# Stores of the gated results: issued by ScalarE with the next gate instead of by GpSimd

## The chip, the cores and the metric

One Trainium2 chip, one of its cores. The metric is the device time of one execution in microseconds (us); the median of three runs stands for a kernel. Engines are named as the profile names them: PE is TensorE (PEld its weight loads), DVE is VectorE, ACT is ScalarE, POOL is GpSimd, SP is SyncE. A "q" behind a name (SPq, ACTq, POOLq) is the engine's sequencer, which issues DMAs.

## The reference, cut to what matters

Linear attention with a decaying state over 4 x 768 tokens and 8 heads of 64, then two feed-forward stages on the 3072 x 512 result. All data are float32 or wider.

```python
state = gamma * state + k[t] v[t]^T ;  y[t] = scale * q[t] @ state     # attention
a = x @ w1 ; b = x @ w2                                                 # 512 -> 1024
h = a * b @ w3 ; x = h @ w_out                                          # 1024 -> 1024 -> 512
h = x @ w_in ; g = h * sigmoid(1.702 * h) ; out = g @ w_out2            # 512 -> 2048 -> 512
```

The change lies around the gate `a * b`, while its results are written to DRAM for the product with `w3 @ w_out`, which the kernel has multiplied into one matrix.

## The kernel before

**Tiling.** Every float32 operand is split into a high and a low float32r part, and each product is three matmuls (`mm3`, lines 245 to 248). The 3072 tokens are six blocks of 512; the gate is computed block by block in the order 0, 2, 4, 1, 3, 5 (`ORDER`). A block has eight gates `t` = 0 to 7, one per 128 rows of the 1024. A gate (`gate_mm`) is 24 matmuls of 128x512 into two PSUM tiles `ab` (`a` and `b`), taken from a pool of six (`mm`, `bufs=6`), so three gates fit in PSUM.

**What happens to a gate.** `gate_out` (lines 283 to 285) copies `ab[0]` to SBUF on ACT and multiplies by `ab[1]` on DVE. The product that follows is a seven-product block scheme (Strassen's kind), which needs sums and differences of blocks. Blocks 0, 2, 4 only store their gates (`gate_first`). Blocks 1, 3, 5 form differences with the stored ones (`gate_second`, lines 1011 to 1025). The eight gates of such a block make four pairs. The even gate of a pair gives `b12` (ACT copy, DVE product) and one difference `g[:, 1]` (DVE, line 1018). The odd gate gives `g[:, 0]`, then `g[:, 3]` on DVE (line 1021), `g[:, 2]` and `g[:, 4]` on POOL (lines 1022, 1023), and the DMA of the whole tile `g` (5 x 512 floats in each of 128 partitions, 1280 KB) to `hd` in DRAM, issued by POOL (line 1024). There are 3 x 4 = 12 pairs; here they are called p1 to p12, p1 to p4 of block 1, p5 to p8 of block 3, p9 to p12 of block 5. The tile `g` has two buffers: p3 can be written only when the store of p1 has landed.

**What runs beside it.** The order of every engine is the order in which the program calls it. Between the matmuls of a gate and `gate_second`, `work(n)` puts in `n` steps that convert the weights of the last stage: ACT takes the magnitude (line 128), DVE does eight operations on two tiles (lines 183 to 205), and then `seven` gives POOL four sums and differences (`four`, line 159) and three stores (line 148). ACT also casts the high part of the next block's `x` (`split`, line 261) and DVE its low part (line 162). SP issues the loads: `h` of the next pair (line 1008, into one of two buffers that POOL's line 1023 reads last), raw weights (line 118), `x` (line 266). At the end of block 5, `opening` and `blend` load the stored blocks again (`l`, `h` from `hd`, line 796) and the product with the mixed matrix begins (PSUM tiles `m`).

In the program each DMA that SP or ACT issues takes one of eight semaphores in turn, and so does each DMA of POOL, from another eight; a DMA waits until the earlier one on its semaphore has landed.

Of the kernel before, what the change touches and what calls it, by code (L numbers as in the profile page):

```python
# [24 lines left out]
KD, KF, KG = DM // P, DF // P, DG // P  # L25
# [18 lines left out]
def tile_kernel(  # L44
# [14 lines left out]
    nc = tc.nc  # L59
# [15 lines left out]
    def spool(name, n, *shape):  # L75
        return [dram.tile(shape, F32, name=f"{name}{i}", tag=f"{name}{i}") for i in range(n)]

    xd = spool("xd", NB, CPB, P, KD, P)
    hd = spool("hd", NB // 2, P, NM, 7, TB)
# [86 lines left out]
    def seven(i, a1, a2):  # L166
        st = (
            st_ready.pop()
            if st_ready
            else homes["st"].tile([P, 1024], F32, tag="st", bufs=2, name="st")  # L170
        )
        four(st, a1, a2)
        store_parts(i, a1, a2, st)
# [66 lines left out]
    def weight(i):  # L240
        while complete <= i:
            work(1)
        return parts[i]

    def mm3(ps, wh, wl, xh, xl, start, stop):
        nc.tensor.matmul(ps, wh, xh, start=start, stop=False, skip_group_check=True)  # L246
        nc.tensor.matmul(ps, wh, xl, start=False, stop=False, skip_group_check=True)  # L247
        nc.tensor.matmul(ps, wl, xh, start=False, stop=stop, skip_group_check=True)  # L248
# [15 lines left out]
    def reload(key, d):  # L264
        lo = x_tiles(key)[1][:, d].bitcast(F32)
        nc.sync.dma_start(
            lo.rearrange("p (c t) -> p c t", c=CPB), xd[key][:, :, d].rearrange("c p t -> p c t")
        )

    def split_x(key, d):  # L270
        hi, lo = (t[:, d] for t in xhl[key])
        split(hi, lo, lo.bitcast(F32))

    def gate_mm(t, key, tile):
        w = [x.rearrange("p (m k f) -> p m k f", m=2, k=KD) for x in weight(t)]
        xh, xl = xhl[key]
        ab = [tile() for _ in range(2)]
        for m, ps in enumerate(ab):
            for d in range(KD):
                mm3(ps, w[0][:, m, d], w[1][:, m, d], xh[:, d], xl[:, d], d == 0, d == KD - 1)  # L280
        return ab

    def gate_out(out, ab):
        nc.scalar.copy(out, ab[0])
        nc.vector.tensor_tensor(out, out, ab[1], ALU.mult)

    def h_tile():
        return xs.tile([P, 2, TB], F32, tag="h", bufs=2, name="h")
# [525 lines left out]
    def opening(t):  # L814
        if t:
            name = blends[t - 1][1]
            wm[name] = wtile("wg")
            nc.sync.dma_start(
                wm[name][1].bitcast(F32), sm[PART[name]].rearrange("p k c -> p (k c)")
            )  # L820
        if t == 1:
            x = spare.tile([P, 7, TB], F32R, tag="ope", name="h0")
            hi2[0] = x[:, NM:]
            load_h(0, 0, NM, x[:, :NM])
        if t == KF - 2:
            for k in (0, 2):
                load_h(1, k, k + 2, prep.tile([P, 2, TB], F32R, tag="r", bufs=R_BUFS, name="h1"))
        if t in (3, 4, 5):
            split_h(0, t - 3, t - 2, hi2[0][:, t - 3 : t - 2])
        if t == 6:  # L830
            hi2["k3"] = prep.tile([P, TB], F32R, tag="x", bufs=6, name="h3")
            split_h(0, 3, 4, hi2["k3"].rearrange("p (a t) -> p a t", a=1))
        if t in (4, 6):
            split_wm(t // 2 - 2)
# [77 lines left out]
    with tc.manual_schedule():  # L912
# [54 lines left out]
        with (  # L967
            tc.tile_pool(name="ps1", bufs=1, space=PSUM, reuse_waits="tile") as psb,
            ExitStack() as stage,
        ):  # L970
            pb = stage.enter_context(tc.tile_pool(name="b1", bufs=1, reuse_waits="tile"))
            homes.update(dict.fromkeys(("wa", "wc", "st"), pb))
            limit = ALL

            def mixed_bank():
                return psb.tile([P, DM], F32, tag="w", bufs=2, name="psw")

            psw = mixed_bank()
            rows = 0
            pair = None  # L980

            def mix_mm(f):
                h3, l3 = (x.rearrange("p (k f) -> p k f", k=KF) for x in weight(W3 + f))
                ps = psw if f == 0 else mixed_bank()
                for k in range(KF):
                    ho, lo = (
                        x.rearrange("p (k f) -> p k f", k=2)[:, k % 2]
                        for x in weight(WO + k // 2)
                    )
                    mm3(ps, h3[:, k], l3[:, k], ho, lo, k == 0, k == KF - 1)  # L990
                return ps

            def mix_out(f, ps):
                nonlocal pair
                if f % 2 == 0:
                    pair = pb.tile([P, 2, 2, 256], F32, tag="xp", bufs=2, name="xp")
                nc.scalar.copy(pair[:, :, f % 2], ps.rearrange("p (m f) -> p m f", m=2))
                if f % 2:
                    seven(f // 2, *(pair[:, m].rearrange("p a f -> p (a f)") for m in range(2)))

            def gate_tile():
                return psb.tile([P, TB], F32, tag="mm", bufs=6, name="psm")

            hb = []

            def load_b(i, k):
                t = h_tile()
                nc.sync.dma_start(t, hd[i // 2][:, k, :2])
                hb.append(t)

            def gate_second(t, i, ab):
                nonlocal b12, g
                b = hb[0]
                if t % 2 == 0:
                    b12 = first_b.pop() if first_b else b12_tile()
                    g = pb.tile([P, 5, TB], F32, tag="g", bufs=2, name="g")
                    gate_out(b12, ab)
                    nc.vector.tensor_tensor(g[:, 1], b12, b[:, 0], ALU.subtract)
                    return
                gate_out(g[:, 0], ab)  # L1020
                nc.vector.tensor_tensor(g[:, 3], g[:, 0], b12, ALU.subtract)
                nc.gpsimd.tensor_tensor(g[:, 2], g[:, 0], g[:, 1], ALU.subtract)
                nc.gpsimd.tensor_tensor(g[:, 4], b[:, 1], g[:, 2], ALU.subtract)
                nc.gpsimd.dma_start(hd[i // 2][:, t // 2, 2:], g)
                hb.pop(0)

            def b12_tile():
                return pb.tile([P, TB], F32, tag="b", bufs=2, name="b12")

            b12 = g = None  # L1030
            for n, i in list(enumerate(ORDER))[1:]:
                nxt = ORDER[n + 1] if n + 1 < NB else None
                for t in range(KF):
                    if nxt is None:
                        opening(t)
                    elif t < 2:
                        for d in range(2):
                            reload(nxt, 2 * t + d)
                    if n > 2 and t % 2 == 0 and t + 2 < KF:
                        load_b(i, t // 2 + 1)  # L1040
                    if n >= 2 and nxt is not None and t == KF - 2:
                        load_b(nxt, 0)
                    ab = gate_mm(t, i, gate_tile)
                    if nxt is not None and t in range(KD - 1, KF - 1):
                        split_x(nxt, t - KD + 1)
                    work(((8, 6, 3, 3)[n - 1] + (n < 4) * (t % 2)) if n < 5 else (t < 4) + (t < 5))
                    (gate_second if n > 2 else gate_first)(t, i, ab)
                    while rows < KF and (complete > W3 + rows or (n, t) == (2, KF - 1)):
                        ps = mix_mm(rows)
                        work(7)  # L1050
                        mix_out(rows, ps)
                        rows += 1
                        if rows == KF:
                            stage.close()
                            pb = homes["st"] = stage.enter_context(
                                tc.tile_pool(name="b2", bufs=1, reuse_waits="tile")
                            )
                            st_ready = [pb.tile([P, 1024], F32, tag="st", bufs=2, name="st")]
                            first_b = [b12_tile()]
                            pb.tile([P, 1024], F32, name="gap")  # L1060
        inner.close()
        homes["st"] = second.enter_context(
            tc.tile_pool(name="wa", bufs=1, side="right", reuse_waits="tile")
# [135 lines left out]
```

## Time and profile before

| | us |
|---|---|
| median of 3 runs | 980.32 |
| lowest and highest | 978.99, 987.53 |
| the profiled execution | 985.11 |
| its span, first to last instruction | 983.3 |
| PE busy in the span | 965.2 |
| DVE, ACT, POOL busy | 714.1, 444.0, 205.6 |

The profile is one execution. Its own time is 985.11 us, of which 983.3 us are the span that all views show; 1.81 us lie around it. Times in the rows are microseconds from the span's start. The stage of the change, from the first `g` to the last store, runs from about 275 to 404 us.

### The profile page before, as it was taken

Reading aid. Unit: us, or ns where it says so; the run is one execution under the profiler, and the core shown is the slowest. Engines: PE = TensorE matmul, PEld = TensorE weight load, DVE = VectorE, ACT = ScalarE, POOL = GpSimd, SP = SyncE. Lnnn points to the kernel's source line nnn. Section 1 sums busy time; section 2 is a strip of 40 time slices with the busy share of each in tenths; the row PEclk is TensorE's granted clock in tenths of the full one; section 3 lists DMA queues with packets and bytes.
Section 4 is the critical chain, followed back from the end, with each engine's and each line's share of the span. In section 5 each row is a group of like instructions: output and inputs, shape, how many; then the busy total and the mean of one; then the engine's idle time right before and its main releaser. Section 6 shows DMA issues by size and latency. Waiting matters only on the chain.

```text
span 983.3 us, 14857 instructions
## 1 busy us (share of the span) xinstructions
PE 965.2 (98%) x5608; PEld 836.4 (85%) x5608; DVE 714.1 (73%) x965; ACT 444.0 (45%) x787; POOL 205.6 (21%) x248
## 2 busy tenths in 40 slices
PE   6999999999999999999999999999999999999998
PEld 5788878888888888778889999999999888888886
DVE  4878878888898896675786895867777475567662
ACT  5666644443322222455446744545545544354430
POOL 5010000278785875240110000000000000000000
PEclk9999999999999999999999999999999999999999
DMA  9889955669898989978767647465596968767871
GB/s 360 336 330 352 356 207 197 216 232 339 315 324 326 347 311 367 404 269 295 271 238 288 250 169 278 180 227 230 197 363 251 331 227 286 243 195 247 287 236 54
DMA packets 115288, 268.73 MB, mean 273 GB/s; under 512 B 8000, under 2 KB 69440, under 8 KB 106128
## 3 DMA queue, kind: packets, MB, share of 16 engines
q1 hardware_dynamic: 100688, 193.98, 56.3%
q0 software_dynamic: 14384, 73.61, 19.3%
q8 instruction: 44, 0.72, 0.3%
q14 instruction: 28, 0.23, 0.1%
q10 hardware_dynamic: 144, 0.20, 0.1%
HBM read 165.52 MB, written 102.24 MB: 272 GB/s over the span
## 4 chain that ended last, share of the span: by engine, by line
PE 89%; DVE 5%; DMA 2%; ACT 1%; issue 1%; POOL 0%; DVEq 0%; ACTq 0%; POOLq 0%
PE m L247 11%; PE m L248 11%; PE m L246 11%; PE psm L246 7%; PE psm L248 7%; PE psm L247 7%; PE a L247 4%; PE a L246 4%; PE a L248 4%; PE y L404 2%; PE s L354 2%; PE e L246 2%; PE e L248 2%; PE e L247 2%; PE psg L246 2%; DMA l<-hd 2%
## 5 line engine op out<-in xcount | busy, mean ns | idle before, releaser
L246 PE MATMUL psm<-xh,wh 128*128 128x512 f32 x320 | 124.6, 389 | 0.0
L248 PE MATMUL psm<-xh,wl 128*128 128x512 f32 x320 | 124.5, 389 | 0.0
L247 PE MATMUL psm<-xl,wh 128*128 128x512 f32 x320 | 124.5, 389 | 0.0
L246 PE MATMUL m<-h,op 128*128 128x512 f32 x320 | 124.5, 389 | 0.0
L248 PE MATMUL m<-h,op 128*128 128x512 f32 x320 | 124.5, 389 | 0.0
L247 PE MATMUL m<-l,op 128*128 128x512 f32 x304 | 118.3, 389 | 0.0
L685 ACT CAST h<-l 128x2048 fp32r<-128x2048 f32 x38 | 72.3, 1914 | 82.8 <-PE m L248 57.4
L686 DVE TENSOR_TENSOR l<-l,h 128x2048 fp32r<-128x2048 f32 x38 | 85.6, 2286 | 20.8 <-ACT h L685 20.8
L247 PE MATMUL a<-yl,op 128*128 128x384 f32 x256 | 85.6, 335 | 0.1
L246 PE MATMUL a<-yh,op 128*128 128x384 f32 x256 | 85.6, 334 | 0.0
L248 PE MATMUL a<-yh,op 128*128 128x384 f32 x256 | 85.5, 334 | 0.0
L691 POOL DMA_DIRECT2D op<-sw x6 | 3.2, 532 | 393.1 <-PE a L248 212.8
L128 ACT ACTIVATE x<-raw 128x512 f32<-128x512 f32 x72 | 46.4, 671 | 75.3 <-DMA raw<-in_wo_dram 43.9
L246 PEld LDWEIGHTS m<-h,op 128*128 128x128 f32 x320 | 60.1, 188 | 12.6
L248 PEld LDWEIGHTS psm<-xh,wl 128*128 128x128 f32 x320 | 60.1, 188 | 12.6
L247 PEld LDWEIGHTS psm<-xl,wh 128*128 128x128 f32 x320 | 60.1, 188 | 12.5
L248 PEld LDWEIGHTS m<-h,op 128*128 128x128 f32 x320 | 60.1, 188 | 12.4
L246 PEld LDWEIGHTS psm<-xh,wh 128*128 128x128 f32 x320 | 60.1, 188 | 12.4 <-issue 0.2
L247 PEld LDWEIGHTS m<-l,op 128*128 128x128 f32 x304 | 57.1, 188 | 11.7
L246 PE MATMUL m<-h,wh 128*128 128x512 f32 x168 | 66.0, 393 | 0.2 <-ACT h L261 0.2
L162 DVE TENSOR_TENSOR l<-l,h 128x2048 fp32r<-128x2048 f32 x19 | 43.6, 2292 | 30.9 <-ACT h L261 30.1
L248 PE MATMUL m<-h,wl 128*128 128x512 f32 x168 | 65.9, 392 | 0.0
(165 smaller groups left out, 2209.5 us busy)
## 6 DMA issues: line engine op xcount, KB each, us to landing
gd<-g SPq DMA_DIRECT2D x32, 1344.0 KB, 4.7
qkv<-in_qkv_dram POOLq DMA_DIRECT2D x20, 1024.0 KB, 8.8
l<-gd SPq DMA_DIRECT2D x26, 768.0 KB, 6.8
l<-hd SPq DMA_DIRECT2D x19, 1024.0 KB, 6.5
raw<-in_w_dram SPq DMA_DIRECT2D x30, 512.0 KB, 5.0
hd<-g POOLq DMA_DIRECT2D x12, 1280.0 KB, 9.1
raw<-in_wo_dram SPq DMA_DIRECT2D x24, 512.0 KB, 7.0
l<-gd SPq DMA_DIRECT2D x24, 512.0 KB, 5.3
```

What stands on the lines that cost most here:

```text
L128: nc.scalar.activation(x, high, AF.Abs, scale=2.0**16)
L162: nc.vector.tensor_tensor(lo, x, hi.bitcast(F32), ALU.subtract)
L246: nc.tensor.matmul(ps, wh, xh, start=start, stop=False, skip_group_check=True)
L247: nc.tensor.matmul(ps, wh, xl, start=False, stop=False, skip_group_check=True)
L248: nc.tensor.matmul(ps, wl, xh, start=False, stop=stop, skip_group_check=True)
L354: nc.tensor.matmul(sc[c][j][:, p, :], qkt[c][r, 1, p, :], qkt[c][r, 0, p, :], start=True, stop=True,)
L404: nc.tensor.matmul(out_y, vs[c][:, 2 * p + j, :], pt[c][:, j, p, :], start=(p < 2), stop=first, skip_group_check=True,)
L685: nc.scalar.copy(hi, x.bitcast(F32))
L686: nc.vector.tensor_tensor(x, x.bitcast(F32), hi.bitcast(F32), ALU.subtract)
L691: queue.dma_start(t.bitcast(F32), sw[PART[name]])
```

## The change

The DMA of `g` is no longer issued in `gate_second` by POOL. It is put in a list, `unstored`, and issued by ACT in the next pair's even gate, right behind ACT's copy of `b12` and DVE's product. The last pair of all (`nxt is None and t == KF - 1`) keeps POOL, and is issued at once behind the loop over blocks.

```diff
-            hb = []
+            hb, unstored = [], []
+
+            def store_g():
+                while unstored:
+                    queue, to, x = unstored.pop()
+                    queue.dma_start(to, x)
...
                     gate_out(b12, ab)
+                    store_g()
                     nc.vector.tensor_tensor(g[:, 1], b12, b[:, 0], ALU.subtract)
                     return
...
                 nc.gpsimd.tensor_tensor(g[:, 4], b[:, 1], g[:, 2], ALU.subtract)
-                nc.gpsimd.dma_start(hd[i // 2][:, t // 2, 2:], g)
+                unstored.append((nc.gpsimd if nxt is None and t == KF - 1 else nc.scalar, hd[i // 2][:, t // 2, 2:], g))
                 hb.pop(0)
...
+            store_g()
         inner.close()
```

Lines behind the change have other numbers in the changed kernel: 1008 becomes 1013, 1018 becomes 1024, 1021 to 1023 become 1027 to 1029, and the store, 1024, becomes 1009.

ACT's order in pairs p4 to p6 before (`b_` is an even gate's copy, `g` an odd gate's, `x` a weight's magnitude, `xh` the cast of the next block):

```order
L284 COPY b_3289<-psm 128x512
L128 ACTIVATE x<-raw 128x512 x2
L284 COPY g<-psm 128x512
L284 COPY b_3381<-psm 128x512
L128 ACTIVATE x<-raw 128x512 x2
L284 COPY g<-psm 128x512
L284 COPY b_3470<-psm 128x512
L261 CAST xh<-xl 128x512
```

ACT's order in the same place after:

```order
L284 COPY b_3288<-psm 128x512
L1009 DMA hd_77<-g 128x2560
L128 ACTIVATE x<-raw 128x512 x2
L284 COPY g<-psm 128x512
L284 COPY b_3380<-psm 128x512
L1009 DMA hd_77<-g 128x2560
L128 ACTIVATE x<-raw 128x512 x2
L284 COPY g<-psm 128x512
L284 COPY b_3469<-psm 128x512
L1009 DMA hd_78<-g 128x2560
L261 CAST xh<-xl 128x512
```

The three DMAs are the stores of p3, p4 and p5; each stands between the even copy of the pair after it and two magnitudes or a cast.

POOL's order from the end of p3 to the start of p4 before (`st` and `sw` are the weight work of `seven`):

```order
L1023 TENSOR_TENSOR g<-h,g 128x512
L1024 DMA hd_77<-g 128x2560
L159 TENSOR_TENSOR st<-x 128x256
L159 TENSOR_TENSOR st<-st,x 128x256
L159 TENSOR_TENSOR st<-x 128x256
L159 TENSOR_TENSOR st<-x,st 128x256
L148 DMA sw_98<-x 128x2x256
L148 DMA sw_98<-x 128x256
L148 DMA sw_98<-st 128x4x256
L1022 TENSOR_TENSOR g<-g 128x512
```

POOL's order in the same place after:

```order
L1029 TENSOR_TENSOR g<-h,g 128x512
L159 TENSOR_TENSOR st<-x 128x256
L159 TENSOR_TENSOR st<-st,x 128x256
L159 TENSOR_TENSOR st<-x 128x256
L159 TENSOR_TENSOR st<-x,st 128x256
L148 DMA sw_98<-x 128x2x256
L148 DMA sw_98<-x 128x256
L148 DMA sw_98<-st 128x4x256
L1028 TENSOR_TENSOR g<-g 128x512
```

Only the DMA of `g` is gone; everything else stands as it stood. SP's and DVE's instructions and their order are the same in both kernels, and PE's too.

## Rows read from the trace of the kernel before

**Rows 1.** The page, busy time, share of the span, instructions of each engine.

```profile
PE 965.2 (98%) x5608; PEld 836.4 (85%) x5608; DVE 714.1 (73%) x965; ACT 444.0 (45%) x787; POOL 205.6 (21%) x248
```

**Rows 2.** Busy time by stretch; at the end granted clock, DMA share, GB/s.

```profile
core 0: us, PE busy (x) PEld busy (x) DVE busy (x) ACT busy (x) POOL busy (x), PEclk, DMA share, GB/s
270.00:300.00 30.00, 30.00 (x134) 24.86 (x133) 26.72 (x34) 6.20 (x12) 23.77 (x27) 1.00 0.96 342
300.00:320.00 20.00, 20.00 (x90) 16.57 (x89) 18.80 (x24) 6.04 (x11) 12.76 (x16) 1.00 0.81 305
320.00:340.00 20.00, 20.00 (x89) 16.54 (x89) 17.87 (x21) 5.60 (x10) 16.29 (x18) 1.00 1.00 356
...
410.00:415.00 5.00, 3.60 (x9) 2.88 (x10) 3.68 (x4) 0.93 (x2) 0.00 (x0) 0.66 1.01 403
```

**Rows 3.** Waits of PE, 265 to 425 us: total, times, longest.

```profile
PE m L247 <- DVE l L162: 2.5, 2, 1.8
```

**Rows 4.** The store's line 1024: its wait, who waited for it, its landing.

```profile
L1024 POOL DMA_DIRECT2D hd<-g x12: 555/564/712, 285.7 to 403.2; - x12
...
  POOL g L1023: 3.6, 12
...
  ACT g L284: 19.6, 3
  DVE g L1018: 7.4, 4
...
DMA to landing us min/median/max: 7.5/9.1/10.9
```

**Rows 5.** DMA issues of the whole run: size, median us from issue to landing.

```profile
gd<-g SPq DMA_DIRECT2D x32, 1344.0 KB, 4.7
```

**Rows 6.** The one DMA that ACT issues: duration of the issue, ns.

```profile
L744 ACTq DMA_DIRECT2D out_dram<-c x1: 370/370/370, 980.4 to 980.4; - x1
```

**Rows 7.** Timeline of POOL, pairs p3 to p5: start, us, and idle before.

```profile
310.50 1.35 POOL L1023 TENSOR_TENSOR g<-h,g 128x512 f32<-128x512 f32 x1
312.14 0.56 POOL L1024 DMA_DIRECT2D hd<-g  x1 [0.30 <-POOL g L1023]
315.66 0.85 POOL L159 TENSOR_TENSOR st<-x 128x256 f32<-128x256 f32 x1 [2.96 <-DVE x L205]
...
322.71 1.63 POOL L1023 TENSOR_TENSOR g<-h,g 128x512 f32<-128x512 f32 x1
...
333.21 1.62 POOL L1023 TENSOR_TENSOR g<-h,g 128x512 f32<-128x512 f32 x1
```

**Rows 8.** Timeline of ACT, pairs p2 to p6.

```profile
286.44 0.66 ACT L128 ACTIVATE x<-raw 128x512 f32<-128x512 f32 x1 [9.68 <-DMA raw<-in_wo_dram]
...
302.80 0.59 ACT L284 COPY b<-psm 128x512 f32<-128x512 f32 x1 [0.36 <-PE psm L248]
...
308.29 0.59 ACT L284 COPY g<-psm 128x512 f32<-128x512 f32 x1 [1.04 <-PE psm L248]
...
321.94 0.57 ACT L284 COPY g<-psm 128x512 f32<-128x512 f32 x1
324.56 0.59 ACT L284 COPY b<-psm 128x512 f32<-128x512 f32 x1 [2.06 <-PE psm L248]
325.05 0.62 ACT L261 CAST xh<-xl 128x512 fp32r<-128x512 f32 x1
332.57 0.59 ACT L284 COPY g<-psm 128x512 f32<-128x512 f32 x1 [6.90 <-DMA hd<-g]
...
363.17 1.23 ACT L128 ACTIVATE x<-raw 128x512 f32<-128x512 f32 x2
```

**Rows 9.** Timeline of PE: two matmuls that stand 24 apart.

```profile
269.96 0.39 PE L246 MATMUL psm<-xh,wh 128*128 128x512 f32 x1
...
275.40 0.39 PE L246 MATMUL psm<-xh,wh 128*128 128x512 f32 x1
```

**Rows 10.** The chain that ended last: the end of the gates.

```profile
397.74 0.24 PE psm L248
```

## The prediction

> **What bounds the kernel now.** I read the page's busy times first. TensorE (PE) is busy for 965.2 of 983.3 us [rows 1], so a change gains only what PE waits, and loses only what PE is made to wait. Next come the stretches of the stage: from 270 to 340 us PE is busy all the time at full granted clock, while ScalarE (ACT) is busy 6.20 of 30 us, 6.04 of 20 and 5.60 of 20, and VectorE (DVE) 26.72 of 30, 18.80 of 20 and 17.87 of 20 [rows 2]. PE's own waits between 265 and 425 us are 2.5 us in two places [rows 3], and both are after the gates, at the first products with reloaded blocks. Around them the granted clock from 410 to 415 us is 0.66 [rows 2]: 5 x 0.34 = 1.7 us are lost to the lower of the two levels. So the stage has 4.2 us to give at most, and only if the loads at its end come sooner.
>
> **PE's timetable.** All else is measured against it. Two matmuls that stand 24 apart start 5.44 us apart [rows 9]: one gate. The last of the 24 gates of p1 to p12 ends at 397.74 + 0.24 = 397.98 [rows 10]; without idle time, gate n ends at 397.98 - (24 - n) x 5.44. With six PSUM tiles, two a gate, gate n + 3 begins 10.88 us after gate n ends, and by then ACT must have copied gate n; DVE's product has 2.72 us more, 13.60. That cover is real: ACT sat idle for 9.68 us before 286.44 [rows 8], and PE stayed busy for all 30 us around it [rows 2].
>
> **What the change removes.** Eleven issues on GpSimd (POOL) go, each 564 ns behind a gap of 3.6 / 12 = 0.30 us [rows 4]: 11 x 0.86 = 9.5 us of POOL. It buys nothing at the first look: behind the store of p3 POOL waits 2.96 us for DVE's weight step anyway [rows 7], so it waits longer instead. I count 0 for PE, and line 1023 of the next pair ends when it did; at most it would end 0.9 us sooner.
>
> **What it adds on ACT.** Eleven issues. The trace has one DMA issued by ACT, 370 ns [rows 6]: 11 x 0.37 = 4.1 us, beside an ACT that is busy for less than a third of each stretch [rows 2]. On PE 0, at the other end 4.1 us if nothing covered it.
>
> **The wait that moves.** The store must follow POOL's line 1023, which reads and writes the last part of `g`. POOL waited for itself, 0.30 us; ACT reaches the store after the even copy of the next pair, and everything behind it on ACT is held. Pair by pair:
>
> p3: the copy of p4 ends at 302.80 + 0.59 = 303.39 [rows 8], p3's line 1023 at 310.50 + 1.35 = 311.85 [rows 7]. ACT stands 8.5 us. Behind it are two magnitudes (1.23 us together) and the odd copy of p4 (0.59), so that copy ends at 311.85 + 0.37 + 1.23 + 0.59 = 314.04 instead of 308.29 + 0.59 = 308.88 [rows 6, 8]: 5.2 us late. It is gate 8, which ends at 310.94, so the copy is due at 321.82: 7.8 us are left.
>
> p4: the even copy of p5 needs half of gate 9, done at 316.38 - 2.72 = 313.66, and so ends at 314.6. Line 1023 ends at 322.71 + 1.63 = 324.34 [rows 7]: 9.7 us of standing. The odd copy of p5 then ends at 324.34 + 0.37 + 1.23 + 0.57 = 326.51, where it ended at 321.94 + 0.57 = 322.51 [rows 8]: 4.0 us late. It is gate 10, due at 332.70: 6.2 us left.
>
> p5: the even copy of p6 ends at 327.10, line 1023 at 333.21 + 1.62 = 334.83 [rows 7]: 7.7 us. The cast behind it ends at 334.83 + 0.37 + 0.62 = 335.82 instead of 325.67, and the odd copy of p6 at 336.41 instead of 333.16 [rows 8]: only 3.3 us late, since before it waited 6.90 us for the landing of p4's store. It is gate 12, due at 343.58: 7.2 us left. DVE stands for the cast too, but the product it owes for gate 12 is due at 332.70 + 13.60 = 346.30, and the block that is cast is first used by gate 17, which starts at 354.46.
>
> The other eight waits, read in the same way, are shorter, and four of them are nothing or nearly so. So ACT stands for tens of microseconds, and PE sees none of it: I take 0. If nothing covered them, the three would cost 5.2 + 4.0 + 3.3 = 12.4 us (by the unrounded figures); I keep that end for the range.
>
> One rule of the Trainium skill speaks against the change. The rows show POOL idle before each of its 12 stores until its own line 1023 was done [rows 4]: the issuing engine holds the wait. The Trainium skill (DMA: Bandwidth & Descriptors, "Anatomy of one DMA — SWDGE (gpsimd) path") says that the transfer engines do not wait for semaphores, and that the wait happens on the issuing sequencer before dispatch. By the rule ACT stands as above; if the wait rode with the transfer, the three waits would be 0. On PE both come to 0 while the cover holds, and the first rival would fall away under the second.
>
> **The landing.** It was 7.5 to 10.9 us from issue [rows 4]; a store of 1344 KB by SP, in a quieter stage, took 4.7 [rows 5]. Those are my bounds; I take the upper half, since the stage moves 305 to 356 GB/s with its transfer engines 81% busy or more [rows 2]. The issue is no later than before at p3 to p5: ACT issues when line 1023 ends, 0.30 us ahead of POOL's start at 312.14 [rows 7]. A sooner landing shortens what ACT and DVE waited for it, 19.6 + 7.4 = 27.0 us [rows 4], and none of that was on PE's list [rows 3].
>
> The Trainium skill (DMA: Bandwidth & Descriptors, "Issuing engines are not separate DMA queues") says that all issuers share the same 16 transfer engines and that spreading saves only the issue time; by it the landing stays at 9.1 us, which no row here can confirm yet.
>
> **Semaphores and SP.** The stores now take turns with SP's loads on eight semaphores. In the changed order, SP's next DMA on a store's semaphore always stands behind a load or step that waits for a pair at least one later, 10.88 us by PE's timetable, and a store lands in 10.9 at most: 0, or a few tenths. `h` loads still wait for the same POOL line.
>
> **Sum.** On PE: 0 from POOL, 0 from the issues, 0 from the waits, 0 from the landing. The profiled execution stays at 985.11 (983.3 span, 1.81 around it). That execution is 4.79 us above the median of the three runs, and the forecast for the median is 980.3.
>
> **Rivals.**
>
> 1. Slower: lateness adds up. A held ACT delays the magnitudes, these DVE's weight steps, these POOL's `seven` and line 1023, and that the next store on ACT. If each pair hands on its lateness, p4 to p6 are 12.4 us late together; cover takes 6.2, PE idles 6.2, and a stretch of the lower clock like that at 410 us adds 1.7: 980.3 + 7.9 = 988.2. If the six pairs that follow each add 3.3 too, 19.5 more: 1,007.7. For it: DVE is about 90% busy here and POOL already waits for it. Against it: the weight work of one tile spreads over more than one pair, and at p6 the old wait for the landing swallows part. It decides once line 1029 of a pair ends more than 6.2 us later than the rows say. I give it 0.12, five parts of it above 1%.
>
> 2. Slower within 1%: the middle holds, but p8 to p11 end 3.3 us late and the reloads of blocks start as late, where the transfer engines are full. PE's idle time there grows by 3.3 and the lower clock comes a second time, 1.7: 985.3. Against it: the p6 wait for the landing resets the lateness. 0.13.
>
> 3. Faster: stores land sooner, the reloads follow sooner, and the 2.5 + 1.7 = 4.2 us at the end of the stage vanish: 976.1. Against it: the last store stays with POOL and the critical reload waits for the last gate. 0.07.
>
> 4. The change gives nothing at all since the landing stays as it was: the forecast's own time, counted with it. The order of the instructions shows that the store does move.
>
> **How the numbers follow.** Forecast (with the fourth) 0.68, rivals 0.12, 0.13, 0.07. The range 976.0 to 988.5 takes in the third, the second and the lower end of the first. Faster by over 1% would mean below 970.5, more than the stage has to give: 0.01. Slower by over 1% means above 990.1, the upper part of the first rival and a share for what I have not seen: 0.06. Within 1%, about what a measurement of this kernel can tell from no change: 0.93.
>
> **What would show it.** Right: PE's waits between 265 and 425 us stay near 2.5 us and its timetable ends the gates near 398; ACT shows idle time of 7 to 10 us ahead of work of pairs p4 to p6 that ends with POOL's line 1029; POOL's busy time falls by some 6 us; odd copies are 3 to 5 us late. Wrong: PE waits for ACT's copy or DVE's product (line 284 or 285) between 300 and 397 us, or the lower clock appears there; or the gates end on time and the reloads (line 796) land later than before.

## The result and the profile after

| | before | after |
|---|---|---|
| median, us | 984.35 (20 runs) | 990.78 (20 runs) |
| lowest run, us | 978.99 | 979.36 |
| profiled execution, us | 985.11 | 992.26 |
| its span, us | 983.3 | 990.5 |

The ratio after to before is 1.006, 95% interval 1.0043 to 1.0077. The change makes the kernel slower, by less than 1%. (With more runs the kernel before has a median of 984.35 instead of the 980.32 of its first three; all its runs but one lie within 8.5 us, which the end of this text comes back to.) That one run, of 1069.96 us, counts as slow and is left out of the ratio. The forecast was 980.3, no change, and 990.8 lies above the range of 976.0 to 988.5.

In the middle of the stage nearly everything went as forecast. The stretches of the changed kernel (columns as in [rows 2]) show PE busy all the time from 300 to 340 us, and from 410 to 415 us a hole where [rows 2] had a small one:

```profile
300.00:320.00 20.00, 20.00 (x90) 16.57 (x89) 18.57 (x24) 5.35 (x10) 12.00 (x14) 1.00 0.79 293
320.00:340.00 20.00, 20.00 (x90) 16.57 (x89) 15.84 (x21) 5.45 (x10) 13.84 (x15) 1.00 1.00 358
410.00:415.00 5.00, 0.32 (x2) 0.00 (x0) 0.00 (x0) 0.00 (x0) 0.00 (x0) 1.00 0.99 406
```

ACT's timeline, pairs p4 to p6 (it answers to [rows 8]; line 1009 is the store, line 1029 was line 1023):

```profile
312.09 0.36 ACTq L1009 DMA_DIRECT2D hd<-g  x1
312.55 1.23 ACT L128 ACTIVATE x<-raw 128x512 f32<-128x512 f32 x2 [9.40 <-POOL g L1029]
313.68 0.58 ACT L284 COPY g<-psm 128x512 f32<-128x512 f32 x1
...
325.03 1.25 ACT L128 ACTIVATE x<-raw 128x512 f32<-128x512 f32 x2 [10.28 <-POOL g L1029]
326.18 0.58 ACT L284 COPY g<-psm 128x512 f32<-128x512 f32 x1
...
335.62 0.62 ACT L261 CAST xh<-xl 128x512 fp32r<-128x512 f32 x1 [8.38 <-POOL g L1029]
336.14 0.58 ACT L284 COPY g<-psm 128x512 f32<-128x512 f32 x1
```

The bracket is the time for which ACT stood before the row, and what released it: 9.40, 10.28 and 8.38 us, each ended by POOL's line 1029, with the store's issue in between. The odd copies end at 314.26, 326.76 and 336.72.

The new store's line (it answers to [rows 4]: its issue in ns, who waited for it, its landing):

```profile
L1009 ACTq DMA_DIRECT2D hd<-g x11: 326/354/361, 286.1 to 396.4; - x11
...
  DVE g L1024: 2.0, 2
  ACT g L284: 0.2, 1
...
DMA to landing us min/median/max: 6.7/7.8/11.1
```

Stores land sooner, and the waits for them fall from 27.0 us to 2.2. None of this shows at PE. What PE waited for between 265 and 425 us is this (it answers to [rows 3]: total, times, longest):

```profile
PE m L246 <- ACT h L261: 7.3, 2, 6.8
PE m L247 <- DVE l L162: 1.5, 1, 1.5
PE m L247 <- DVE h L162: 0.8, 1, 0.8
```

That is 9.6 us, all of it after the gates, which end at 397.55 (397.98 before). From 380 to 440 us PE idles for 2.71 us before (the 2.5 of [rows 3], and 0.2 in a third place, behind ACT's line 261) and for 9.60 after. These 6.89 us are nearly the whole of the 7.15 us between the two executions. (The lower clock adds little. Before, it is 0.66 from 410 to 415 us, while PE is busy for 3.60 us: some 1.2 us lost. After, it is 0.55 from 415 to 420 us with PE busy for 1.35, and 0.77 from 420 to 425 with PE busy throughout: some 1.8 us.)

**Where the 6.9 us come from.** Three loads count, all of line 796 on SP's queue: h0 (`h<-hd`, 1024 KB, issued behind p8's line 1023), h1 (`h<-hd`, two times 512 KB) and l2 (`l<-hd`, 1024 KB, the block for which PE waits). The chain is read best on ACT and SP, kernel before first. ACT before, at p10:

```profile
379.57 0.62 ACT L261 CAST h<-h 128x512 fp32r<-128x512 f32 x1 [10.90 <-DMA h<-hd]
380.10 0.58 ACT L284 COPY g<-psm 128x512 f32<-128x512 f32 x1
```

ACT after, at the same two instructions:

```profile
382.58 0.62 ACT L261 CAST h<-h 128x512 fp32r<-128x512 f32 x1 [14.32 <-DMA h<-hd]
383.10 0.58 ACT L284 COPY g<-psm 128x512 f32<-128x512 f32 x1
```

The cast of h0 stands in ACT's order ahead of the odd copy of p10, so p10 cannot go on until h0 has landed, in either kernel. From the start of this cast to the start of the same pair's line on POOL it is 4.58 us before (384.15) and 4.57 after (387.15). That line frees the buffer into which SP loads `h` of p12, and in SP's order h1 and l2 stand behind this load. SP before:

```profile
385.79 0.32 SPq L1008 DMA_DIRECT2D h<-hd  x1
386.16 0.90 SPq L818 DMA_DIRECT2D wl<-sm  x2
387.23 1.49 SPq L796 DMA_DIRECT2D h<-hd  x2
388.89 0.41 SPq L818 DMA_DIRECT2D wl<-sm  x1
389.58 0.54 SPq L796 DMA_DIRECT2D l<-hd  x1
```

SP after:

```profile
388.79 0.32 SPq L1013 DMA_DIRECT2D h<-hd  x1
389.21 0.93 SPq L818 DMA_DIRECT2D wl<-sm  x2
390.23 3.34 SPq L796 DMA_DIRECT2D h<-hd  x2
393.74 0.64 SPq L818 DMA_DIRECT2D wl<-sm  x1
395.18 0.54 SPq L796 DMA_DIRECT2D l<-hd  x1
```

The chain that ended last, in order of time (start, us, what), now runs through these loads:

```profile
385.28 1.79 POOL g L1028
387.15 1.63 POOL g L1029
388.79 6.30 DMA h<-hd
395.18 19.96 DMA l<-hd
415.16 1.91 ACT h L261
417.09 2.30 DVE l L162
419.44 0.79 PE m L247
```

ACT's cast of l2 starts at 415.16; before it was this row:

```profile
407.11 1.91 ACT L261 CAST h<-l 128x2048 fp32r<-128x2048 f32 x1 [2.17 <-DMA l<-hd]
```

The 8.05 us between them are the sum of four steps. h0 is issued 1.11 us later (366.54 against 365.43). It takes 1.9 us longer to land (16.0 against 14.1). From the end of p10's line on POOL to the issue of l2 it is 2.59 us more (6.41 against 3.82), mostly SP's issue of h1, 3.34 us instead of 1.49; SP then stands another 0.8 us until the `h` load of p12 has landed, at 388.79 + 6.30 = 395.09. And l2 takes 2.45 us longer to land (19.98 against 17.53). The first step alone proves nothing: in the four kernels below that move no store ahead of p9's (p9 to p11, p9, or p10 and p11 on ACT; p9 on SP), h0 is issued anywhere between 363.13 and 366.44 us. The experiments ask what causes the first three steps; why l2 itself lands more slowly was not tried by itself.

### The profile page after: what moved, and what is told of

Same layout as the page of the kernel before. It is cut to its first block, busy times and chain, and to the rows that moved or that the text cites. A ratio compares the mean times of both kernels' runs of the same rounds, so it can differ in the third digit from the quotient of the medians.

```text
span 990.5 us, 14852 instructions
## 1 busy us (share of the span) xinstructions
PE 963.3 (97%) x5608; PEld 834.5 (84%) x5608; DVE 716.8 (72%) x965; ACT 443.3 (45%) x787; POOL 194.0 (20%) x237
## 4 chain that ended last, share of the span: by engine, by line
PE 54%; DVE 3%; DMA 3%; issue 2%; POOL 2%; ACT 1%; DVEq 0%; ACTq 0%; POOLq 0%; SPq 0%
PE m L247 11%; PE m L246 11%; PE m L248 11%; PE a L247 4%; PE a L248 4%; PE a L246 4%; DMA l<-hd 2%; PE e L247 2%; PE e L246 2%; PE e L248 2%; PE c L247 1%; PE c L246 1%; PE c L248 1%; DMA h<-hd 1%; DVE g L583 1%
## 5 line engine op out<-in xcount | busy, mean ns | idle before, releaser
L247 PEld LDWEIGHTS m<-l,op 128*128 128x128 f32 x304 | 57.1, 188 | 11.7
```

## The experiments

Each ratio is to the kernel before, on the same chip, with its 95% interval; it need not be the quotient of the medians. A kernel has one profiled execution, and all details (landings, waits of PE) are from that one. The theories, with the letters that the expectations use: **hold** (H: ACT's standing for POOL delays the chain), **queue** (R: p9's store, beside h0, makes h0 land later when ACT issues it), **semaphore** (S: l2 takes the turn of the `h` load of p12 in the changed kernel, since ACT's stores count in the turns, and must wait for its landing) and **slow issue** (SP's h1 beside ACT's store of p10).

**Only the hold.** POOL keeps all stores. ACT copies one element of the same `g` at the place where the store would stand, which makes it wait for the same line.

```diff
                     gate_out(b12, ab)
+                    while last_g:
+                        nc.scalar.copy(still[:, 1:2], last_g.pop()[:, 4, :1])
...
                 nc.gpsimd.dma_start(hd[i // 2][:, t // 2, 2:], g)
+                last_g.append(g)
```

> POOL keeps all 12 stores; ACT gets, where the changed kernel has the store, a copy of one element of g[:, 4], so it is held by POOL's line 1023 as there, and no DMA moves. Theory H (the held ACT makes pairs p5 to p8 late, the reload h0 starts 1 us late, p10 ends 3 us late, and the reloads behind it come late): ratio to before about 1.006, PE idle time between 395 and 425 us about 9 us instead of 2.7, line 1023 of p10 ends near 388.8. Theory S (the stores' turns on SP's semaphores make the reload l2 wait for a load that was just issued): ratio 1.000 to 1.001, l2 issued near 390 to 391, PE idle below 4 us.

Measured: 986.93, ratio 1.003 (1.0004 to 1.0055). h0 is issued at 366.51 and lands in 14.4 us; h1 takes 1.44 us to issue, p10's line ends at 387.13, and PE waits 5.1 us, less than theory H has it. By its middle the wait alone costs half of the loss; the interval reaches from next to nothing to nearly all of it.

**Which stores.** The condition under which a store goes to ACT is changed; the others are issued by POOL at once. First p1 to p8 on ACT:

```diff
-unstored.append((nc.gpsimd if nxt is None and t == KF - 1 else nc.scalar, hd[i // 2][:, t // 2, 2:], g))
+to = hd[i // 2][:, t // 2, 2:]
+if nxt is not None:
+    unstored.append((nc.scalar, to, g))
+else:
+    nc.gpsimd.dma_start(to, g)
```

> ACT issues the stores of p1 to p8 as in the changed kernel, POOL those of p9 to p12 at once. The holds of p3 to p8 stay, the turns of SP's semaphores at the end are those of before (l2 does not wait for the load of h). Theory H: about 1.004 to 1.006, line 1029 of p10 ends near 388 to 389, l2 issued near 392. Theory S: about 1.000.

Measured: 986.26, ratio 1.0023 (1.0001 to 1.0046); h0 lands in 14.6 us, p10's line ends at 386.44 and l2 is issued at 390.30, both earlier than theory H has them. Then p9 to p11:

```diff
-if nxt is not None:
+if nxt is None and t < KF - 1:
```

> POOL issues the stores of p1 to p8 at once, ACT those of p9 to p11; POOL the last. No hold before p9; l2 takes the semaphore of the load of h that stands eight DMAs ahead of it, as in the changed kernel. Theory S: 1.003 to 1.006, l2 issued only when that load has landed, some 6 us behind line 1029 of p10 instead of 3.8. Theory H: 1.000 to 1.001, PE idle between 395 and 425 us below 4 us.

Measured: 989.19, ratio 1.0049 (1.0018 to 1.0081). h0 takes 16.7 us, l2 is issued 6.50 us behind p10's line, PE waits 7.8 us. With no early hold at all most of the loss is there. The last three stores were split further, by the same edit with other conditions. p9 alone:

```diff
-if nxt is not None:
+if nxt is None and t == 1:
```

> Only the store of p9 is issued by ACT; POOL keeps the other 11. ACT is held at most 1 to 3 us, before it waits for h0 anyway; l2 does not wait for the load of h. Theory R (a store in ACT's own queue takes a share of the transfer engines from SP's loads beside POOL's queue, where POOL's stores follow one another): h0 lands 16 to 17 us after issue instead of 14.1, line 1029 of p10 ends 1.5 to 2.5 us later than before, ratio 1.001 to 1.003. Theory S (semaphores alone): h0 lands after 14.1 us, ratio 1.000.

Measured: 987.36, ratio 1.005 (1.0021 to 1.0078). Its profiled execution, 985.18, was one of its quicker ones; PE waits 3.5 us. h0 in the view of DMA issues (size, us from issue to landing):

```profile
h<-hd SPq DMA_DIRECT2D x1, 1024.0 KB, 14.6
```

p10 and p11 alone:

```diff
-if nxt is not None:
+if nxt is None and t in (3, 5):
```

> ACT issues the stores of p10 and p11 only; l2 stands eight DMAs behind the load of h. Theory S: h0 lands after 14.1 us, line 1029 of p10 ends as before near 386, but l2 is issued 6.3 us behind it, when the load of h has landed, instead of 3.8; ratio 1.002 to 1.004. If only the late h0 counted: 1.000.

Measured: 984.78, ratio 1.0017 (0.9996 to 1.0038). Here h1 takes 3.33 us to issue and l2 comes 6.5 us behind p10's line, so semaphore and slow issue are both there, and PE waits only 0.7 us; but this execution, 980.81, is one of the four quickest of 12, and the others took 984.17 to 986.66. Then the changed kernel with p11 back on POOL, so that l2 no longer has the turn of the `h` load:

```diff
-if nxt is not None:
+if nxt is not None or t < KF - 3:
```

> The changed kernel with p11's store back on POOL, issued at once: l2 stands seven DMAs behind the load of h and takes the semaphore of an older load. Theory S: the gap from the load of h to l2 falls from 6.4 to about 4 us, and the ratio from 1.006 to 1.003 or 1.004. If SP's issues are slow for another reason (next to ACT's store of p10), the gap stays at 5.5 to 6.4 and the ratio at 1.005 to 1.006.

Measured: 991.08, ratio 1.0081 (1.0054 to 1.0108). The semaphore theory falls: without that wait the kernel is no faster. l2 comes 5.91 us behind p10's line, since h1 still takes 3.32 us to issue. (The profiled execution, 987.80, is one of the three quickest of 8.)

**The stores on SP.** SP issues p1 to p10 right behind the load of `h` for a later pair (p11 and p12 by POOL):

```diff
 gate_out(b12, ab)
-store_g()
...
+if nxt is not None or t < KF - 3:
+    unstored.append((nc.sync, to, g))
+else:
+    nc.gpsimd.dma_start(to, g)
...
 load_b(nxt, 0)
+if n > 2 and t % 2 == 0:
+    store_g()
```

> SP issues the stores of p1 to p10, each right behind its load of h, which waits for the same POOL line already; POOL issues p11 and p12 at once. ACT is never held and POOL is rid of 10 issues; l2 stands seven DMAs behind the load of h and does not wait for it. Theory H and theory S: 1.000, PE idle 1 to 4 us. If a store outside POOL's queue slows the loads by itself (theory R: sharing of the transfer engines), 1.003 or more and h0 and l2 land over 15 and 18 us after issue.

Measured: 979.69, ratio 0.9966 (0.9947 to 0.9985): faster than both kernels. h0 lands in 11.0 us, ACT casts l2 at 403.67 without a wait, and PE has no wait between 265 and 435 us. The same with p9 alone on SP, all others on POOL:

```diff
-if nxt is not None or t < KF - 3:
+if nxt is None and t == 1:
     unstored.append((nc.sync, to, g))
```

> SP issues the store of p9 behind its load of h; POOL keeps the other 11. In SP's own queue the store follows h0 and can not take a share from it. Theory R: h0 lands after about 11 us, line 1028 of p10 ends some 3 us sooner than before, ratio 0.997 to 0.999. Otherwise: h0 after 14 us, ratio 1.000.

Measured: 979.72, ratio 0.9981 (0.9966 to 0.9997). h0 in the same view:

```profile
h<-hd SPq DMA_DIRECT2D x1, 1024.0 KB, 11.4
```

Against p9 alone on ACT, 1.005 on the same chip, that is 0.7% for the engine that issues one store, and the two intervals do not touch. So, by the middles of the intervals, one store on ACT costs nearly as much as all eleven (1.006), and the parts do not add up to the whole.

**Without p9's store on ACT, in three ways.** First the changed kernel with p9's store on POOL at once:

```diff
-if nxt is not None:
+if not (nxt is None and t in (1, KF - 1)):
```

> The changed kernel, but the store of p9 is issued by GpSimd at once, as before; p1 to p8, p10 and p11 stay on ScalarE. If the queue of p9's store is what slows the 1 MB reload h0, h0 lands in about 14.5 us (16.0 in the changed kernel), and the ratio falls from 1.006 to about 1.002 or 1.003, what the hold on ScalarE alone gave. If it is the number of held pairs that adds up, whichever queue the stores have, the ratio stays at 1.005 or above, with h0 at about 16 us.

Measured: 987.57, ratio 1.004 (1.0021 to 1.006); h0 in 14.9 us, PE waits 6.4 us. It lies between the two expectations, and the interval reaches to both. p9's store on SP, behind the load for p11, the other ten on ACT:

```diff
-store_g()
+if not (nxt is None and t == 2):
+    store_g()
...
+    unstored.append((nc.sync if nxt is None and t == 1 else nc.scalar, to, g))
...
+if nxt is None and t == 2:
+    store_g()
```

> The changed kernel, but the store of p9 is issued by SyncE behind the loads of p11, in the queue that also holds h0; the other ten stay on ScalarE. If the landing of h0 carries the loss, h0 lands in about 11 us in spite of the ten stores on ScalarE, TensorE waits less than 3 us between 265 and 435 us, and the ratio is 1.000 to 1.002. If the hold, or the slow issue of h1 beside p10's store, carries it, the ratio stays at 1.004 or above and l2 (the second reload of the last block) still lands after 413 us.

Measured: 981.17, ratio 0.9981 (0.9961 to 1.0001). h0's landing, in the view of DMA issues (size, us from issue to landing):

```profile
h<-hd SPq DMA_DIRECT2D x1, 1024.0 KB, 11.1
```

ACT's timeline of the same run at p9 and p10:

```profile
367.11 0.59 ACT L284 COPY b<-psm 128x512 f32<-128x512 f32 x1 [2.75 <-PE psm L248]
...
374.29 0.62 ACT L261 CAST h<-h 128x512 fp32r<-128x512 f32 x1 [6.59 <-DMA h<-hd]
374.81 0.58 ACT L284 COPY g<-psm 128x512 f32<-128x512 f32 x1
```

The holds at p3 to p5 are still there (6.79, 8.41 and 8.10 us), h1 still takes 2.54 us to issue, and PE waits for nothing between 265 and 435 us. So in this execution neither costs PE anything; that they cost only when h0 lands late is argued from it. The execution, 979.36, is the quickest of 12, five of which took 984.14 to 986.27. The third way leaves the stores on ACT and takes away most of the hold: p1 to p8 on ACT, behind the odd copy, p9 to p12 on POOL.

```diff
                     gate_out(b12, ab)
-                    store_g()
...
                 gate_out(g[:, 0], ab)
+                store_g()
...
```

> ScalarE stores p1 to p8, but behind its odd copy of the next pair, so that it hardly stands for GpSimd (under 4 us at a time instead of 8 to 10); p9 to p12 are stored by GpSimd at once. If the hold on ScalarE is what made the same stores cost 1.0023 when issued behind the even copy, the ratio is now 0.999 to 1.001 and line 1029 of p8 ends near 364.5 us. If ScalarE's queue as such, beside the loads, costs the time, the ratio stays at 1.002. A later store also lands later: if that becomes the wait, ScalarE or VectorE waits for the landing at the even gates and the ratio is above 1.003.

Measured: 980.91, ratio 0.9984 (0.9958 to 1.001). Against 1.0023 with the hold (the same eight stores) it agrees with the hold theory, though the intervals overlap and the chips differ; p8's line on POOL ends at 363.05. In the profiled execution, 979.92 (five of 12 took 982.64 to 990.67), h0 landed in 11.7 us with p9's store on POOL, where five other kernels with that store on POOL needed 13.9 to 14.9. So the queue of p9's store is not all that sets this landing.

**The chain itself.** All stores stay as the change has them. Only the splits of h0 into high and low parts are called one gate later, so that ACT's first cast of h0 stands behind the odd copy of p10.

```diff
-        if t in (3, 4, 5):
-            split_h(0, t - 3, t - 2, hi2[0][:, t - 3 : t - 2])
-        if t == 6:
+        if t in (4, 5, 6):
+            split_h(0, t - 4, t - 3, hi2[0][:, t - 4 : t - 3])
+        if t == 7:
...
```

> The changed kernel with all its stores as they are; only the four high and low parts of h0 are made one gate later, so that ScalarE's first cast of h0 stands behind the odd copy of p10 instead of ahead of it. If the loss runs from h0's landing through that cast into p10's line 1029 and the loads that follow it, then p10's line 1029 ends at about 381 us or sooner (388.77 in the changed kernel) although h0 still lands in 14 to 16 us, the second reload l2 is issued before 391 us, TensorE waits less than 3 us between 265 and 435 us, and the ratio is 0.996 to 1.000. If the loss comes from the transfers as such (full transfer engines beside ScalarE's queue), l2 still lands after 413 us and the ratio stays at 1.004 or above. A third way: the casts that are made later become late themselves, and TensorE waits for them at the first products after 397 us.

Measured: 980.17, ratio 0.9971 (0.9953 to 0.9989), runs from 979.67 to 981.09. ACT's timeline, odd copy of p10 and cast:

```profile
372.61 0.59 ACT L284 COPY g<-psm 128x512 f32<-128x512 f32 x1 [4.85 <-PE psm L248]
380.79 0.62 ACT L261 CAST h<-h 128x512 fp32r<-128x512 f32 x1 [7.59 <-DMA h<-hd]
```

POOL's last step of p10, in its timeline:

```profile
378.05 1.29 POOL L1029 TENSOR_TENSOR g<-h,g 128x512 f32<-128x512 f32 x1
```

h0 lands in 14.9 us (16.0 in the changed kernel, 14.1 before), but p10 does not hang on it: p10's line ends at 379.34 instead of 388.77, l2 is issued at 391.78 and cast at 404.52, and PE waits 0.7 us. The chain that ended last has these two pieces:

```profile
379.37 12.33 DMA h<-hd
391.78 12.72 DMA l<-hd
```

l2 still waits for the `h` load of p12, so it is issued only 3.40 us sooner than in the changed kernel; the other 7.2 of the 10.64 us by which its cast comes sooner are a shorter landing, 12.7 us instead of 20.0. The loads ahead of it on SP's queue went out sooner; that this is why it lands sooner is argued, not shown.

The other kernels fit. In the 13 that cast h0 ahead of p10's copy, l2's cast follows h0's: the seven that cast h0 before 380 us cast l2 at 403.01 to 407.11, the six that cast h0 after 380 us cast l2 at 407.28 to 415.16. Here h0 is cast at 380.79, and l2 at 404.52. So it is shown that the loss passes through h0's cast in front of p10's copy: with all eleven stores on ACT and that cast behind the copy the kernel is faster than before. What makes h0 late is shown in part, by p9's store; the mechanism of it stays open. The kernel before with the later casts was not run, so what the change costs or gains once the cast is out of the way is not known.

## Why the prediction was wrong

**PE's timetable: right.** The gates end at 397.55, forecast 397.98; PE never waited for line 284 or 285.

**What the change removes: right in effect.** POOL's busy time fell by 11.6 us (205.6 to 194.0, forecast some 6), and nothing in the run shows a gain from it. But line 1023 of the next pair did not end when it did: up to p5 it was within 0.5 us, at p6 1.6, at p8 1.1 and at p10 3.0 us later.

**What it adds on ACT: right.** 326 to 361 ns an issue, forecast 370.

**The wait that moves: right about the wait, wrong about its price.** Forecast 8.5, 9.7 and 7.7 us of standing, measured 9.40, 10.28 and 8.38; forecast odd copies at 314.04, 326.51 and 336.41, measured 314.26, 326.76 and 336.72. The other eight were not all shorter: p8's, the pair behind which h0 is loaded, was 8.69. The price of 0 was measured against PSUM alone. The later a held pair ends, the later SP's next loads go, and this cover was not counted. p8's line ended 1.11 us later than before in the profiled executions, far less than the 3.3 us of the second rival. The kernel with the hold alone loses 0.3%, with an interval from 0.04 to 0.55%.

**The landing: half right.** ACT's stores landed sooner, 7.8 us against 9.1, and their waits fell to 2.2 us. The step looked at the stores and not at what moves beside them. h0 took 16.0 us instead of 14.1, l2 19.98 instead of 17.53. The Trainium skill (DMA: Bandwidth & Descriptors, "Issuing engines are not separate DMA queues") has the issuing engines share the transfer engines, with only issue time to be saved. The trace agrees on the sharing: from 362 to 384 us the queues of SP, ACT and GpSimd take 39.4, 30.3 and 20.7% of the transfer engines' time. But the choice of queue also went with the landing of a neighbour: h0 took 14.6 to 16.7 us with p9's store on ACT, 11.0 to 11.4 on SP behind the load.

**Semaphores and SP: the step that failed.** It asked only whether a DMA waits for its turn of a semaphore, and ended with "`h` loads still wait for the same POOL line". They do, and that is the path. In the kernel before, ACT already stood 10.90 us for h0 ahead of p10's copy, and l2, for which PE waits 1.8 of the 2.5 us of [rows 3], already stood behind p10's line in SP's order. The prediction saw the 2.5 us of [rows 3] but did not follow them back to what paced them. Had it done so, each 1 us on h0 would have counted as 1 us on p10's line and on what SP issues behind it: in the runs h0 came 3.0 us later, p10's line 3.0, l2 8.05, and PE idled 6.89 us more. So the terms of 0 for the waits and the landing fail there, and its own sign of being wrong came in: the gates ended on time and the reloads landed later. The semaphore turn it priced at "a few tenths" exists (SP stood 0.8 us before l2), and freeing l2 of it made the kernel no faster.

**The sum: the start was off as well.** Of the 10.5 us between the forecast of 980.3 and 990.8, 4.0 are the start: the first three runs have a median of 980.32, twenty have 984.35. The change itself makes 6.4. A range of the same width about the better median would have taken 990.8 in, by luck, since the path was missed all the same.

**Rivals.** The second had the right place, the reloads at the end of the stage, and too small a size: 985.3, by 3.3 us at p8 to p11 and 1.7 of the clock. In fact 1.11 us at p8 grew to 8.05 at l2 along the chain, and PE's idle time grew by 6.89. Its argument against itself, that the old wait for the landing resets lateness, is not borne out: at p6 the line ended later, by 1.6 us where it had been 0.3 at p5. The first rival's lateness did not add up: under holds of 50.2 us in all PE stayed busy to the end of the gates. The third, 976.1, named the gain that comes when the reloads are early, and the kernels that made them early reach it in part: 0.9966 and 0.9971 of the time before. The chances by size stand better than the range: 0.6% is within the 1% that a measurement can tell.

## What to carry to other kernels

Before an issue or a wait is put on another engine, look in the timelines for an instruction there that already waits for a load ahead of work that frees the next loads; lateness passes through such a place in full (3.0 us here), while idle time and PSUM cover say nothing of it. A small wait at the end of a stage is to be followed back to the instruction that paces it, also through the order of SP's queue. Here moving that one cast behind one copy (0.9971) was worth about as much as the best choice of queue for the stores (0.9966, ten of them on SP).

## What the runs showed that was not expected

- **A store's queue and a neighbour's landing.** h0, 1024 KB on SP's queue, landed in 11.0, 11.4 and 11.1 us with p9's store behind it on the same queue, in 11.7 to 14.9 us with it on POOL's, and in 14.6 to 16.7 us on ACT's. Each number is one execution, and the last two groups touch; why the queues differ was not tried.
- **SP's issue of h1 and a store of ACT.** The two issues of h1 took 3.25 to 3.34 us in five kernels with p10's store on ACT, 2.54 in the sixth, and 0.95 to 1.69 in six kernels with it on POOL; with it on SP they took 2.15. The seventh with it on ACT, the one with the later casts, has 1.10: there h1 is issued 4.6 us behind that store instead of 1.4. That the store is what slows the issue is not shown.
- **The spread of the runs goes with this chain.** The kernel before ran from 979.29 to 987.36 in 17 runs on the chip of the last experiment, the kernel with h0's cast one gate later from 979.67 to 981.09 in 12, and the two that store p9 alone or ten pairs on SP from 978.37 to 981.85 in 24 (on other chips). The changed kernel has one run of 20 at 979.36, as quick as any before. That the low end of the old spread is made of runs in which h0 landed early enough is argued from this, since only one execution of each kernel has a trace.
